# Another written-out order of all steps, with other early loads and fewer constant products

## The chip, the cores and the metric

The kernel runs on one NeuronCore of a Trainium2 chip. Five engines work side by side, each with its own instruction queue that runs in order: TensorE (PE; its weight loads are listed apart, as PEld), VectorE (DVE), ScalarE (ACT), GpSimd (POOL) and SyncE (SP), which here only issues DMA transfers. The metric is the time of one execution on the device in microseconds (us).

## What is computed

A recurrence over 768 time steps for 4 x 8 heads of width 40 is followed by a feed-forward block with an exact GELU, d_model 320 and d_ff 2048:

```python
for t in range(S):
    y[:, :, t] = np.einsum('bhd,bhde->bhe', rt, state)
    Sa = np.einsum('bhde,bhe->bhd', state, at)
    state_decay = state * wt[:, :, None, :] - np.einsum('bhd,bhe->bhde', Sa, bt)
    state = state_decay + np.einsum('bhd,bhe->bhde', vt, kt)
...
x = y.transpose(0, 2, 1, 3).reshape(B * S, H * D)
h = x @ w_in
g = 0.5 * h * (1.0 + erf(h * inv_sqrt2))
return g @ w_out
```

The six inputs of the recurrence are 32-bit floats. The two weights come as 64-bit floats, so that each is 5.2 MB and has to be turned into 32-bit numbers on the chip.

## The kernel before

The time axis is cut into 12 chunks of 64 steps. Within a chunk the recurrence becomes matrix products, with the inverse of a triangular matrix for each of the 32 heads. Chunk c's result x goes through the feed-forward block while the following chunks are being prepared.

Every piece of work is a named step, a small Python function. The order in which steps are issued is written out by hand as one long list of names in the function `order`. The number behind the name is the chunk (for the conversion steps, the unit). The kernel walks through the list and performs each; a step puts its instructions at the end of the queues of the engines that it uses. So the place in the list fixes the order on every engine's queue at once, and also which of four PSUM banks a product gets: `take` gives out the bank that has been free longest, `drop` returns it, in the list's order. A step at the head of a queue that is not ready holds everything behind it on that queue. Semaphore waits between engines follow from what steps read and write.

```python
def perform(steps, token):
    name, *numbers = token.split(".")
    steps[name](*(int(n) if n.isdigit() else n for n in numbers))
...
    for token in order(NCH, NS):
        perform(steps, token)
```

The steps that matter here, by what they do:

- **Loads, on SP's queue.** `Lw`, `La`, `Lb`, `Lk`, `LV`, `Lr` load a chunk's rows of the inputs w, a, b, k, v, r (lines 417 to 476). `Lf` and `Lf5` load the 64-bit words of w_in (lines 512 and 522), in 20 pieces of 256 KB, named by block of rows, half and part; `Ls` loads those of w_out (line 545). `Ns` and `Nl` take the triangular matrices through DRAM into GpSimd's layout (lines 852, 860), `Is`, `If` and `Ij` bring the inverses back (lines 880, 887, 892). `ox` exchanges rows of x between partitions (lines 1130, 1133), `so` stores results (line 1294).
- **Preparing a chunk.** `lg` takes the logarithm of w (ScalarE, line 645), `wT` and `cu` are products with a triangle of ones (TensorE), `ew` and `ec` the exponentials of these (ScalarE, lines 670 and 688). `ec` writes the decays that `sb` (VectorE, line 730) and `sk` (GpSimd or VectorE, line 735) multiply into the rows of b and k. `ta`, `tb`, `tk`, `tr`, `tv` transpose; `sa`, `sn`, `kc`, `rc`, `vc` scale or copy what they give.
- **The triangular matrices.** `nm` is the product (TensorE), `nk` its masking (VectorE, line 811); likewise `vm` with `vk` and `am` with `ak`.
- **The inverse in the first chunk.** It is computed by squarings: `qm.0` to `qm.4` on TensorE, each followed by `qc` (ScalarE), `qz` and `qa` (VectorE); `qt` and `qi` prepare it, `ql` and `qx` end it.
- **The inverse in the other chunks.** GpSimd clears its tile (`iz`, line 864) and eliminates row by row (`ic`, lines 873 and 875, eight steps in a chunk). When the inverses of 32 x 32 blocks are back, `tc_` (VectorE, line 961), `jm`, `jc`, `km`, `kt0` and `kt1` join the blocks.
- **The chunk's result and state.** `av`, `xm`, `sm`, `pk`, `pb`, `ym`, `tm` on TensorE, `xc0`, `xc1`, `sc`, `oa`, `om`, `od`, `oc`, `tn`, `yc` on VectorE and ScalarE. `om` writes x.
- **The feed-forward block.** `mh` is x @ w_in (line 1185), eight steps of 20 products for a chunk, `ge` the GELU (line 1190). The product with w_out is `pm` (line 1301) in the first three chunks and later the seven products `m1` to `m7` of a Strassen scheme (line 1224) with sums `s1` to `s4`, `e1` to `e6`.
- **Conversion of the 64-bit words**, in units (0 to 9 for w_in, 10 to 25 for w_out). Exponent and mantissa are taken apart by `cp`, `cm`, `cs` (VectorE) and `ce` (ScalarE), and put together in one of three ways: by `cv` alone (two VectorE instructions), by `cl`, `cn` (ScalarE) and `cg` (two GpSimd instructions), or, for unit 0, by `cx` on TensorE and `cy` on VectorE.
- **Products of constants.** `warm_first` (three) and `warm.4.i` (one each, 512 columns; i is only a label) multiply constants and nobody reads the result; they keep TensorE busy while it would wait.
- **Clearing of pads**: `pads_*`, `first_ones`, `Tt_zero`, `bias_set`, `unused` and the masks, nearly all on GpSimd.

Of the kernel before, what the change touches and what calls it, by code (L numbers as in the profile page):

```python
# [1339 lines left out]
```

## Time and profile before

| | |
|---|---|
| median of 3 runs | 688.01 us (685.67 to 690.76) |
| the profiled execution | 684.3 us, of which the span is 682.6 |
| TensorE busy | 652.3 us (96%) |
| VectorE, GpSimd, ScalarE busy | 385.2, 377.2, 236.9 us |
| mean granted TensorE clock | 0.989 |
| moved by DMA | 74.26 MB |

The page and the trace are of one execution. In rows of instructions, the first number is the start in us from the span's beginning, the second the duration; L1185 is a line of the kernel. In the brackets at the end stand the idle time of that engine just ahead of the row, and what ended it. The granted clock is the share of full speed that TensorE was given. "issue" is time in which an engine waited for nothing that the profile shows.

### The profile page before, as it was taken

The page shows a single profiled execution, that of the slowest core. Times are in us where ns is not written, and L with a number is a line of the kernel's source. Part 1 is how long each engine was busy: PE and PEld are TensorE (multiplying, and loading weights), DVE is VectorE, ACT ScalarE, POOL GpSimd, SP SyncE. Part 2 cuts the span into 40 slices and gives each one's busy share as a digit, 9 for nine tenths or more (in the row PEclk, how much of TensorE's full clock was granted, in tenths as well). Part 3 has the DMA queues.
Part 4 walks back from the last instruction along what each step waited for, and adds up shares of the span by engine and source line. Part 5 has one row for each costly group of instructions (what it writes and reads, how often), then busy time and mean ns, then how long its engine had stood idle before and what let it go on. Part 6 is the DMA issues. An engine that isn't in the chain of part 4 may idle for free.

```text
span 682.6 us, 29596 instructions
## 1 busy us (share of the span) xinstructions
PE 652.3 (96%) x13250; PEld 569.6 (83%) x13250; DVE 385.2 (56%) x483; ACT 236.9 (35%) x313; POOL 377.2 (55%) x796
## 2 busy tenths in 40 slices
PE   8687999999999999999989989999999999999997
PEld 4476887788778778998988988997998998998987
DVE  1868989750833645781852853753952763624403
ACT  4547535526222325322323332432342332132020
POOL 3445854853857705871883874864873863840000
PEclk9987999999999999999999999999999999999999
DMA  9987668758668746458547766656767153140100
GB/s 157 161 163 161 129 165 176 131 97 145 111 127 126 150 82 125 95 102 129 110 83 138 126 118 120 129 95 125 131 123 142 35 100 68 31 71 16 26 15 21
DMA packets 286043, 74.26 MB, mean 109 GB/s; under 512 B 265660, under 2 KB 280796, under 8 KB 285916
## 3 DMA queue, kind: packets, MB, share of 16 engines
q1 hardware_dynamic: 284852, 69.84, 55.2%
q0 software_dynamic: 864, 2.36, 2.0%
q8 instruction: 104, 1.70, 1.1%
q14 instruction: 23, 0.19, 0.1%
q10 hardware_dynamic: 200, 0.16, 0.1%
HBM read 58.69 MB, written 9.70 MB: 100 GB/s over the span
## 4 chain that ended last, share of the span: by engine, by line
PE 62%; POOL 14%; SPq 8%; DMA 6%; DVE 5%; issue 4%; ACT 1%; POOLq 0%; DVEq 0%
PE bank L1185 24%; PE bank L194 17%; PE bank L1224 14%; POOL tmp L873 7%; POOL W L875 6%; PE bank L1301 6%; SPq L417 2%; PE bank L697 1%; DMA w_out_sb<-in_moe_w_in_dram 1%; DMA Nb<-N_blocks 1%; DMA inv_blocks<-W 1%; SPq L522 1%; DVE conv L589 1%; SPq L887 1%; DMA r_pairs<-in_r_dram 1%
## 5 line engine op out<-in xcount | busy, mean ns | idle before, releaser
L1185 PE MATMUL bank<-xt,w_in_sb 64*128 64x256 f32 x1920 | 221.0, 383 | 1.8 <-issue 1.6
L873 POOL TENSOR_TENSOR tmp<-W,Nb 128x126 f32<-128x126 f32 (+22 forms) x341 | 152.7, 448 | 122.5 <-DMA Nb<-N_blocks 96.7
L1185 PEld LDWEIGHTS bank<-xt,w_in_sb 64*128 64x128 f32 x1920 | 185.7, 188 | 25.3 <-issue 4.2
L875 POOL TENSOR_TENSOR W<-W,tmp 128x126 f32<-128x126 f32 (+22 forms) x341 | 155.6, 456 | 26.7
L1190 ACT ACTIVATE gt<-bank 128x1024 f32<-128x1024 f32 x48 | 48.9, 1022 | 139.9 <-PE bank L1185 138.7
L1224 PE MATMUL bank<-w_out_sb,gt 128*128 128x160 f32 x576 | 82.8, 301 | 0.0
L1224 PEld LDWEIGHTS bank<-w_out_sb,gt 128*128 128x128 f32 x576 | 79.1, 190 | 1.3 <-issue 0.3
L1301 PE MATMUL bank<-w_out_sb,gt 128*128 128x320 f32 x192 | 54.9, 439 | 1.4 <-DVE w_out_sb L598 0.8
L1301 PEld LDWEIGHTS bank<-w_out_sb,gt 128*128 128x128 f32 x192 | 35.6, 190 | 16.4 <-DVE w_out_sb L598 1.3
L1062 DVE TENSOR_TENSOR SM<-bank,upper 128x832 f32<-128x832 f32 x24 | 23.7, 1016 | 29.2 <-PE bank L194 29.2
L961 DVE STREAM_TRANSPOSE conv<-Tt 128x512 f32<-128x512 f32 x11 | 7.8, 707 | 43.6 <-DMA Tt<-inv_blocks 43.5
L1112 DVE TENSOR_TENSOR st<-bank,st 128x832 f32<-128x832 f32 (+1 forms) x22 | 20.9, 985 | 16.8 <-PE bank L194 16.8
L1010 DVE COPY Tt<-bank 32x512 f32<-32x512 f32 x9 | 6.2, 689 | 41.6 <-ACT Tt L1010 41.5
L1177 DVE TENSOR_TENSOR os<-os,bank 128x160 f32<-128x160 f32 x36 | 11.5, 318 | 26.8 <-PE bank L1224 18.9
L1224 PE MATMUL bank<-extra,conv 128*128 128x160 f32 x176 | 26.0, 301 | 0.0
L1224 PEld LDWEIGHTS bank<-extra,conv 128*128 128x128 f32 x176 | 24.3, 190 | 0.5
L811 DVE TENSOR_TENSOR VR<-bank,upper 128x1024 f32<-128x1024 f32 x12 | 14.6, 1217 | 15.2 <-PE bank L194 15.1
L1177 DVE TENSOR_TENSOR conv<-gt 128x1024 f32<-128x1024 f32 x9 | 11.3, 1257 | 20.5 <-ACT gt L1190 20.4
L1043 DVE COPY SM<-bank 128x832 f32<-128x832 f32 x10 | 10.1, 1013 | 21.1 <-PE bank L194 21.1
L575 ACT ACTIVATE conv<-conv,rebias 128x320 uint32<-128x320 uint32 (+1 forms) x26 | 15.8, 619 | 18.0 <-DVE conv L568 17.9
L864 POOL MEMSET W<- 128x512 f32 x11 | 5.8, 529 | 29.1 <-DMA inv_blocks<-W 29.1
L1079 ACT COPY st<-bank 128x1024 f32<-128x1024 f32 x11 | 11.1, 1013 | 29.9 <-PE bank L194 29.9
(207 smaller groups left out, 1096.9 us busy)
## 6 DMA issues: line engine op xcount, KB each, us to landing
Nb<-N_blocks SPq DMA_DIRECT2D x22, 256.0 KB
b_rows<-in_b_dram SPq DMA_DIRECT2D x24, 160.0 KB
VR<-in_v_dram SPq DMA_DIRECT2D x24, 160.0 KB
k_rows<-in_k_dram SPq DMA_DIRECT2D x24, 160.0 KB
out_dram<-os SPq DMA_DIRECT2D x48, 80.0 KB
Tt<-inv_blocks SPq DMA_DIRECT2D x44, 64.0 KB
a_pairs<-in_a_dram SPq DMA_DIRECT2D x18, 144.0 KB
r_pairs<-in_r_dram SPq DMA_DIRECT2D x36, 72.0 KB
```

The lines of the kernel that those rows point to most:

```text
L194: nc.tensor.matmul(o, lhsT, rhs, start=first, stop=True, skip_group_check=True)
L575: nc.scalar.activation(power, power, ACT.Relu, bias=rebias, scale=8.0)
L811: nc.vector.tensor_tensor(to, pt, upper.unsqueeze(1).to_broadcast([P, NBL, C]), ALU.mult)
L873: nc.gpsimd.tensor_tensor(t, W[:, :rows, j:j + 1].to_broadcast([P, rows, rest]), Nb[:, j:j + 1, j + 1:].to_broadcast([P, rows, rest]), ALU ...
L875: nc.gpsimd.tensor_tensor(W[:, :rows, j + 1:], W[:, :rows, j + 1:], t, ALU.add)
L1062: nc.vector.tensor_tensor(SM[:, g], pair_of(f"S{c}_", g).rearrange("p x i c -> p i x c"), pass_upper.unsqueeze(1).unsqueeze(1).to_broadcas ...
L1112: nc.vector.tensor_tensor(to, pair_of(f"QY{c}_", g)[:, :, :, cols], to, ALU.add)
L1177: nc.vector.tensor_tensor(to, one_, other, how)
L1185: nc.tensor.matmul(ph[:, x, s], w_in_sb[half(x), kt, p * P:(p + 1) * P], xt[half(x), kt], start=kt == 0, stop=kt == NK - 1)
L1190: nc.scalar.activation(gt[:, 4 * q:4 * q + 4].rearrange("p (x s) t -> p x s t", x=2), bank(f"ph{c}_{q}").rearrange("p x (s t) -> p x s t", ...
L1224: nc.tensor.matmul(po[:, n, :DM // 2], l_[:, f], r_[:, f], start=f == 0, stop=f == NF // 2 - 1)
L1301: nc.tensor.matmul(po[:, g, :DM], gt[:, f, g * P:(g + 1) * P], w_out_sb[:, f], start=f == 0, stop=f == NF - 1)
```

## The change

Only the list in `order` is altered: nearly every line of it is another. No function is added or removed, and each step does what it did. Compared as lists:

- **Steps left out or added.** Before, eight single products of constants (`warm.4.` 20, 5, 29, 7, 24, 8, 1, 0); after, six (12, 5, 17, 10, 11, 20). Unit 1 of the conversion ends with `cl.1`, `cn.1`, `cg.1` instead of `cv.1`, unit 25 the other way round. All others, 1,470 of some 1,480, are in both lists.
- **The first loads.** Before, four pieces of w_in stand between w and b of the first chunk, and the rest of w_in lies among rows of the first two chunks. After, w.0, b.0 and w.1 come first, a.0 behind one piece, then the other pieces of the first part of w_in in one run, and b.1 and a.1 behind them.
- **The rest.** The engines' queues are reordered throughout, mostly by a few places.

The beginning of the list, cut:

```diff
-        pads_a.1 pads_a.0 Lw.0 Lf.0.1.0 lg.0 warm_set identity sums_mask first_ones.1 warm.4.20 warm_first
-        Lf.0.0.0 pads_w.1 bias_set pads_r.0 pads_extra.2 pads_extra.3 first_ones.0 pads_rows.1 pads_w.0
-        pads_extra.0 pads_rows.0 upper_mask pads_r.1 iz.1 pads_extra.1 cm.0 cn.0 wT.0 warm.4.5 cu.0 ec.0 cl.0
-        cx.0 ew.0 Lf.1.1.0 Lf.1.0.0 Lb.0 La.0 sb.0 cp.1 tb.0 cp.0 ce.0 sn.0 ta.0 sa.0 nm.0 Lw.1 Lb.1 Lf.2.1.0
-        Lf5.0.1 Lf.2.0.0 ce.1 lg.1 cm.1 nk.0 qi cu.1 wT.1 warm.4.29 ec.1 cs.0 cy.0 qt qm.0 cs.1 sb.1 cp.2 cm.2
+        pads_extra.0 sums_mask Lw.0 lg.0 cu.0 ec.0 pads_VR.0 identity Lb.0 warm.4.12 sb.0 tb.0 pads_w.0
+        first_ones.0 Lw.1 lg.1 warm_set bias_set pads_w.1 wT.1 pads_a.0 upper_mask pads_extra.1 Lf.3.0.0 La.0
+        Lf.2.0.0 wT.0 ew.1 ew.0 sn.0 pads_a.1 pads_r.0 ta.0 sa.0 nm.0 nk.0 qt qi Lf.0.1.0 Lf.1.0.0 Lf5.0.0
+        Lf.0.0.0 Lf5.0.1 Lf.1.1.0 cp.0 cu.1 ec.1 ce.0 cs.0 warm_first qm.0 cm.0 qc.0 cp.1 ce.1 cn.0 qz.0 cm.1
+        warm.4.5 Lf.2.1.0 cl.2 cn.1 cl.0 cs.1 qm.1 qa.1 qz.1 cx.0 Lf.3.1.0 cl.1 qc.1 Lb.1 La.1 qm.2 first_ones.1
...
```

Later places that the prediction speaks of. On GpSimd, before: `ic.5` (all) `Is.5 sk.5 iz.6`; `ic.6 Is.6 sk.6 iz.7`; `ic.7 Is.7 sk.7 iz.8 sk.8 ic.8`; `sk.9` inside `ic.9`; `Is.9 sk.10 iz.10 ic.10`. After: `sk.5` inside `ic.5`; `Is.5 sk.6 iz.6`; `Is.6 sk.7 iz.7`; `Is.7 iz.8 sk.8 ic.8`; `Is.8 iz.9 sk.9 ic.9`; `ic.10 Is.10 sk.10 iz.11`. On SP, before: `Is.1.0 Ns.2.1 Ls.13 Is.1.1 Ls.15 Nl.2.1 If.1.1 Ls.10 If.1.0`; after: `Is.1.0 Ls.13 Is.1.1 Ls.15 Nl.2.0 If.1.0 Nl.2.1 If.1.1 Ls.10`. And before: `Ns.7.1 If.6.1 If.6.0 Ij.6.0 so.4.0 Nl.7.0 Ij.6.1 Nl.7.1`; after: `so.4.1 Ns.7.0 Ns.7.1 Nl.7.0 Nl.7.1 Ij.6.1 If.6.1 If.6.0 LV.7 so.4.0`.

## The prediction

> **What bounds the kernel now.** I read the page's forty slices first, for the engine that never rests. Rows are TensorE's busy tenths, its granted clock and the share of the DMA engines.
>
> ```profile
> PE   8687999999999999999989989999999999999997
> PEclk9987999999999999999999999999999999999999
> DMA  9987668758668746458547766656767153140100
> ```
>
> TensorE is the bound from the fifth slice on: 652.3 us busy of a 682.6 us span. The change alters the set of products by two constants only, so it can win or lose just where TensorE waits or runs at a lower clock. Hence the second view, the start in windows of 4 us (window, length, busy time of PE, PEld, DVE, ACT, POOL, granted clock, DMA share, GB/s).
>
> ```profile
> 32.00:36.00 4.00, 1.33 (x81) 1.07 (x72) 1.74 (x2) 0.56 (x2) 3.30 (x4) 1.00 1.18 125
> 36.00:40.00 4.00, 4.00 (x74) 3.24 (x66) 2.75 (x4) 1.23 (x2) 0.40 (x1) 0.57 0.83 174
> ...
> 52.00:56.00 4.00, 2.20 (x128) 2.00 (x128) 4.00 (x5) 3.23 (x5) 2.05 (x3) 0.68 0.66 157
> 56.00:60.00 4.00, 3.32 (x84) 3.13 (x84) 3.51 (x6) 2.58 (x4) 0.60 (x1) 0.50 0.78 146
> ```
>
> Idle windows are followed by windows of a low clock: 4 x 0.43 + 4 x 0.32 + 4 x 0.50 = 5.0 us of TensorE's time gone. The timeline says who is late there: the first chunk's inversion, squaring after squaring (nm.0, qm.0, qm.1, qm.4).
>
> ```profile
> 18.61 1.16 PE L194 MATMUL bank<-aT,nT 40*64 40x64 f32 x64 [1.51 <-DVE aT L719]
> ...
> 24.62 1.19 PE L194 MATMUL bank<-N,st 32*32 32x32 f32 x116
> ...
> 30.95 1.58 PE L194 MATMUL bank<-turned,st 32*32 32x64 f32 x97
> ...
> 53.45 1.70 PE L194 MATMUL bank<-turned,st 32*32 32x32 f32 x108
> ```
>
> I summed TensorE's steps at their undisturbed durations (mh 2.2 us, pm 4.5, nm 1.05, and so on) in the old and the new order. The old order has done 34.5 us of work by 57.1 us, the new one stands within some 3 us of the old at nearly every milestone, and the whole is 629.6 us against 627.5. Next I looked at where the saturated stretch is met by a chain that is just in time: the second chunk's inversion, from GpSimd's last row to the product jm.1.
>
> ```profile
> 95.19 0.35 POOL L875 TENSOR_TENSOR W<-W,tmp 128x16 f32<-128x16 f32 x1
> 100.67 0.67 SPq L880 DMA_DIRECT2D inv_blocks<-W  x1
> 111.88 0.98 SPq L892 DMA_DIRECT2D T<-inv_blocks  x2
> 114.87 0.70 DVE L961 STREAM_TRANSPOSE conv<-Tt 128x512 f32<-128x512 f32 x1
> 115.62 0.75 PE L194 MATMUL bank<-conv,spare 32*32 32x32 f32 x64 [0.39 <-DVE conv L961]
> ```
>
> GpSimd was done at 95.5 and TensorE waited at 115.6: nearly all between is the SP queue. Last, the waits of the steady part. Only two have a releaser that is a step of the kernel and are over 1 us: both are `ec` (line 688), held by `sk` (line 735).
>
> ```profile
> 403.37 1.63 POOL L880 DMA_DIRECT2D inv_blocks<-W  x2 [0.30 <-POOL W L875]
> 404.95 1.60 POOL L735 TENSOR_TENSOR k_rows<-k_rows,part 128x640 f32<-128x640 f32 x1
> 406.59 0.70 ACT L688 ACTIVATE part<-bank 128x640 f32<-128x640 f32 x1 [5.33 <-POOL k_rows L735]
> 407.34 1.16 PE L194 MATMUL bank<-aT,nT 40*64 40x64 f32 x64 [1.74 <-ACT part L688]
> ```
>
> sk.7 sits behind all of ic.7; ec.8 must wait for it, and nm.8 needs the PSUM bank that ec.8 frees. The other is vm.7 behind ec.7 and sk.6, 1.76 us at 356.5. The clock then reads 0.92 and 0.91 in 400 to 410 and 410 to 420: 10 x (0.08 + 0.09) = 1.7 us more.
>
> **The change, part by part.** The profiled execution took 684.3 us, 1.7 over its span, and lies 3.7 under the median of 688.0. I add terms to it and carry the sum to the median.
>
> *Order of the loads.* Counting the SP queue, the new order has 0.64 MB issued up to b.0 (old 1.66), 0.96 up to w.1 (2.30), 1.54 up to a.0 (1.98), but 4.16 up to b.1 (2.62) and 6.27 up to v.0 (5.38); from the 76th issue on the two queues are level. Path to nm.0: lg.0 ends at 8.14 as before; cu.0 1.25; ec.0 0.70; then lg.1 with its table load 2.02, the exponential's table load 1.28, ew.1 and ew.0 2.0, sa.0 1.23. That is 16.7 against 18.61. nk.0 takes 1.22 more, `qi` on GpSimd 6.43, so qm.1 can start at 25.5 against 30.95. Further on the late rows end the lead's growth. The old queue passes 6.21 MB at 39.7, and a load of k took 5.3 us from issue to its reader (35.7 to 41.0), so v.0 is there at 45. tv.0 (1.97) and tk.0 (1.0) now stand ahead of qm.4, which starts at 48 instead of 53.5. Lead: 5 us. VectorE's conversions, begun at 8.3 us before, begin at about 21; what slides is 1.7 us of cp and cm, and unit 1 gives back 1.37 by passing to ScalarE and GpSimd (unit 25 returns 1.0 late, beside full TensorE work). I cost both at nothing: VectorE idles 3.6 us in 20 to 40 and 3.2 in 40 to 60. If that cover is gone, it is 1.7 us at most.
>
> *What of the lead reaches jm.1.* ic.1 took 33.4 us from 62.1 on; its input Nl.1.0 is the 67th issue instead of the 65th, 1.3 us later. Is.1.0 is the 118th instead of the 116th (+1.3), but the 2.5 us that the queue stood before xt's exchange (71.4 to 73.9, waiting for om.0) go with the lead: 99.5. From there the old queue needed 11.2 us to its last inverse load; the new one has Ls.13, Is, Ls.15, two Nl and the If together: Is.1.1 lands at 105.4, the If are out at 107.4, and with the 3.0 us between the old queue's last If (111.8) and tc_.1, jm.1 starts at 111.2: -4.4 us. TensorE's 85.5 us of work before it (86.5 before) is done by then. Bounds: -7 if GpSimd is also earlier, +4 if om.0 and nk.1, for which the queue now waits, are late.
>
> *Constants.* Eight single ones become six (the three of warm_first stay). Three of the eight stand in full stretches, at 60.1, 80.9 and 123.6 us, about 1.1 each by start to start; in the new order one does. Before jm.1 the chain decides, so only the one behind it counts: -1.0.
>
> *sk ahead of the inversion.* sk.6 to sk.9 move ahead of their ic, sk.5 into ic.5. Both ec waits go: -1.76 - 1.74 - 1.7 = -5.2 us. sk.10 goes behind ic.10 instead; ec.11 then holds a bank that mh.9.6 takes, with av.10 and ym.10 (2.5 us) between. I take nothing, at most 1.8.
>
> *What is late next.* TensorE arrives earlier at every jm. Their slack (from tc_'s start to jm's, less tc_) is small: chunk 2 0.8, 3 2.9, 4 0.9, 5 2.2, 7 1.4, 9 4.8. The work between nm and jm shrinks by 1.8 in chunk 2, 2.3 in 5, 2.2 in 7, 5.6 in 9. Chunk 2 waits 1.0. Chunk 5, with sk.5's 1.6 inside, 1.7. Chunk 7 would wait most, but its Nl, which stood behind so.4.0 and left at 363.5, now stands ahead of it and of the If: ic.7 can start some 6 us earlier. Chunk 9 has sk.9 out of its middle. Given back: +2.7.
>
> Sum: -4.4 - 1.0 - 5.2 + 2.7 = -7.9; 676.4 for a profiled run, **680 us** for the median.
>
> [...] The row: after the 2.67 us idle at 32.5 the clock was 0.57, and after 48 to 56, busy 2.2 to 2.3 of each 4 us with no idle over 1.7 us, 0.68 and 0.50. [...]
>
> **Rivals.**
> 1. *The clock falls more in the start.* With fewer constants and TensorE held at tv.0 from about 41 to 45 us, the low windows double: another 5.0 us. Against: the squarings stand closer. 688.0 - 7.9 + 5.0 = 685.
> 2. *The lead is lost on SP and GpSimd.* ic.1 starts no earlier and the queue is level from the 76th issue, so jm.1 stays at 115: 688.0 - 3.5 = 684.5. For it: GpSimd's 33.4 us and SP's unbroken issuing from 0 to 100 us. Against: 11.2 us from Is to the last load.
> 3. *Slower: the inversion ends last in every chunk whose window shrank.* Where Nl does not land before GpSimd is free, TensorE waits 1.0, 1.7, 4.3 (2.2 + 3.5 - 1.4) and 0.8 us in chunks 2, 5, 7 and 9, and the clock falls behind each as at 407, 4 x 1.7. With no gain at the start: 688.0 - 1.0 - 5.2 + 7.8 + 6.8 = 696. For it: Nl was what GpSimd waited for, 96.7 us in 10 waits. It decides from a Nl landing some 2 us later than now.
> 4. *Nothing changes*, each wait replaced by its like: 687. For it: TensorE's sequence is the old one within a few us nearly everywhere.
>
> **How the numbers follow.** Forecast 0.46 (own range 673 to 686), rival 1 0.12, rival 2 0.16, rival 3 0.20, rival 4 0.06. About 1% (6.9 us) is what a measurement of this kernel tells from no change, so faster is below 681.1 and slower above 694.9. Faster: some two thirds of the forecast and a quarter each of rivals 1 and 2, 0.38. Slower: rival 3 with a tenth of the rest, 0.27. The same: 0.35. The range leaves out a tenth on each side: 671 to 698.
>
> **What would show it.** qm.4 before 50 us and the If of chunk 1 out by 108 bear out the start; jm.1 at 115 or later with ic.1 ending at 97 or later is rival 2. No wait for ec over 1 us near vm.7 and nm.8 bears out the sk term; waits on tc_, Js or T in chunks 2, 5, 7 or 9 are rival 3. Clock under 0.9 in more than three windows before 64 us is rival 1. VectorE still converting w_in when mh.0 is due would make all of it wrong.

## The result and the profile after

The changed kernel takes 693.69 us (median of 20 runs, 686.84 to 699.21) beside 687.74 us for the kernel before in the same session: a ratio of 1.008, 95% interval [1.0061, 1.0099]. The forecast was 680, faster; it came out slower by 0.8%. The runs of the changed kernel lie further apart here, 12.4 us from end to end against 5.1, but in later sessions the kernel before spread by up to 13 us too. In the tables below a median is of all runs of a kernel and a ratio of its fast runs alone (within 1.5% of its fastest), so the two do not always agree, and the one profile of a slow run (without_two_nl9) is left out of the means. The profiled execution took 694.07 us, its span is 692.1 against 682.6, and the mean granted clock 0.979 against 0.989.

The forty slices of the page after (TensorE's busy tenths, its granted clock, DMA's share):

```profile
PE   4789899999999999999999999999998989999997
PEclk9996999999999999999999999999999999999999
DMA  9999578847569556559547757446755643130000
```

TensorE is still the bound, with 652.4 us of busy time as before (652.3), though it has two constants fewer: its products ran slower, not more of them. The clock's dip is deeper in slice 4 (52 to 69 us), and there is a new dent in TensorE's row at slices 31 and 33. These are the two places where the time went. The first, in windows of 4 us (columns as in the prediction):

```profile
32.00:36.00 4.00, 4.00 (x54) 1.58 (x57) 2.22 (x4) 0.59 (x1) 1.49 (x2) 0.61 0.75 150
...
52.00:56.00 4.00, 2.90 (x42) 1.34 (x46) 1.40 (x2) 1.80 (x4) 3.84 (x4) 0.52 0.91 110
56.00:60.00 4.00, 4.00 (x82) 2.38 (x77) 1.89 (x3) 1.35 (x3) 1.73 (x4) 0.50 0.79 145
60.00:64.00 4.00, 4.00 (x136) 3.82 (x134) 2.45 (x4) 1.48 (x3) 0.00 (x0) 0.50 0.81 187
...
92.00:96.00 4.00, 4.00 (x94) 3.40 (x88) 3.96 (x8) 1.04 (x2) 3.45 (x8) 0.64 0.69 194
```

Before, TensorE had one stretch of 6.8 us at half clock in the fifties (53.4 to 60.2); in windows of 0.2 us it now lasts 13.7 us, from 52.2 to 65.8 (the expectations below take it as 13.2), and another of 3.4 us comes at 93. From 53.1 on TensorE is full in these windows, so every us in them costs half a us. The timeline of TensorE shows how the stretch begins and what is done in it:

```profile
49.12 1.09 PE L193 MATMUL bank<-turned,st 32*32 32x32 f32 x104 [0.68 <-DVE turned L944]
53.10 0.54 PE L193 MATMUL bank<-turned,st 32*32 32x32 f32 x24 [2.89 <-issue]
53.57 2.08 PE L193 MATMUL bank<-cum_m,ident 128*128 128x512 f32 x2
55.57 1.99 PE L193 MATMUL bank<-aT,kT 40*64 40x64 f32 x64
57.49 2.07 PE L193 MATMUL bank<-cum_m,ident 128*128 128x512 f32 x2
```

qm.4 starts at 49.1, as early as forecast (48), but stops inside its 128 products for 2.89 us on "issue". Then follow two products of constants (one is two rows of the trace), am.0 and vm.0, each at nearly double length: a constant takes 2.08 us instead of 1.12. jm.1 starts at 120.46 instead of 115.62.

The second place is SP's queue while chunk 8 is being finished. First the kernel before, then after (start, duration, number of issues):

```profile
455.31 3.20 SPq L852 DMA_DIRECT2D N_blocks<-spare  x4
...
464.38 0.47 SPq L860 DMA_DIRECT2D Nb<-N_blocks  x1
464.90 1.24 SPq L1294 DMA_DIRECT2D out_dram<-os  x2
466.18 0.60 SPq L860 DMA_DIRECT2D Nb<-N_blocks  x1
```

```profile
466.21 2.05 SPq L851 DMA_DIRECT2D N_blocks<-spare  x4
468.30 1.04 SPq L891 DMA_DIRECT2D T<-inv_blocks  x2
469.39 1.17 SPq L1293 DMA_DIRECT2D out_dram<-os  x2
470.67 3.99 SPq L439 DMA_DIRECT2D w_tile<-in_w_dram  x4
474.77 2.25 SPq L859 DMA_DIRECT2D Nb<-N_blocks  x2
```

Ns.9 (N_blocks) now stands behind the inverse loads If.8, and Nl.9 (Nb) behind the stores so.6.0 and the loads Lw.10 as well, so Nl.9 leaves at 474.8 instead of 464.4. GpSimd waits 14.94 us for it (7.73 before) and starts ic.9 at 480.6 instead of 470.3 (GpSimd's first row of ic.9, before and after):

```profile
470.27 0.24 POOL L873 TENSOR_TENSOR tmp<-W,Nb 128x31 f32<-128x31 f32 x1 [7.73 <-DMA Nb<-N_blocks]
```

```profile
480.61 0.24 POOL L872 TENSOR_TENSOR tmp<-W,Nb 128x31 f32<-128x31 f32 x1 [14.94 <-DMA Nb<-N_blocks]
```

Two waits of TensorE come of it, the second in part, as will be shown (VectorE's row first, then TensorE's two):

```profile
524.12 0.71 DVE L960 STREAM_TRANSPOSE conv<-Tt 128x512 f32<-128x512 f32 x1 [10.10 <-DMA Tt<-inv_blocks]
...
525.80 0.75 PE L193 MATMUL bank<-conv,spare 32*32 32x32 f32 x64 [2.73 <-DVE SM L1042]
564.47 10.43 PE L1184 MATMUL bank<-xt,w_in_sb 64*128 64x256 f32 x80 [2.59 <-ACT part L687]
```

The first of TensorE's is jm.9: VectorE had stood 10.10 us for the inverse (tc_.9), with the copy that the bracket names behind it. The second is mh.9.6, which needs the bank that ec.11 frees, which waits for sk.10 behind all of ic.10. Behind each the clock reads 0.83, in the windows 520 to 530 and 560 to 570, which is 1.7 us each. The two waits and the two dips come to 2.7 + 2.6 + 1.7 + 1.7 = 8.7 us, most of what is lost in this part.

The middle did get faster. The table gives the starts of jm as read from TensorE's timeline of several kernels, and what lies between; in each column the order of the steps is either that of before (b) or that of after (a).

| kernel | jm.1 | jm.2 to jm.7 | jm.7 to jm.11 | jm.11 to the end |
|---|---|---|---|---|
| before | 115.6 b | 254.5 b | 203.2 b | 60.5 |
| after | 120.5 a | 250.4 a | 216.1 a | 60.5 |
| after, second profile | 121.8 a | 249.0 a | 214.4 a | 60.5 |
| start_of_after | 121.7 a | 254.3 b | 203.2 b | 60.5 |
| start_of_before | 116.9 b | 251.7 a | 215.5 a | 60.5 |
| middle_of_after | 116.7 b | 248.5 a | 204.7 b | 60.5 |
| only_nl9 | 118.2 a | 251.3 a | 210.7 a, Nl.9 early | 60.5 |
| two_constants_later | 117.6 a, constants moved | 250.3 a | 214.8 a | 60.5 |
| both_kept_ns | 115.7 a, constants moved | 249.2 a | 207.1 a, Ns.9 and Nl.9 early | 60.5 |

The new order has less work done by jm.1, jm.2 and jm.7 (1.0, 4.3 and 4.3 us, counted with undisturbed durations as in the prediction), so starts alone flatter it in the first half. Against work done it lies 5.8 us behind at jm.1, 4.9 at jm.2, 0.9 at jm.7 and 11.6 at the end; less the 2.1 us of constants left out, that is the 9.5 us between the spans. So, in this profile: some 5 lost in the start, 4.0 won from jm.2 to jm.7, 10.7 lost from there on.

### The profile page after: what moved, and what is told of

The parts are those of the page before. It is cut to its first block, busy times and chain, and to the rows that moved or that the text cites. A ratio compares the mean times of both kernels' runs of the same rounds, so it can differ in the third digit from the quotient of the medians.

```text
span 692.1 us, 29580 instructions
## 1 busy us (share of the span) xinstructions
PE 652.4 (94%) x13246; PEld 569.4 (82%) x13246; DVE 388.2 (56%) x483; ACT 240.6 (35%) x316; POOL 377.7 (55%) x796
## 4 chain that ended last, share of the span: by engine, by line
PE 70%; POOL 10%; DVE 6%; issue 5%; DMA 4%; SPq 3%; ACT 2%; DVEq 0%; POOLq 0%; ACTq 0%
PE bank L1184 24%; PE bank L193 22%; PE bank L1223 16%; PE bank L1300 8%; POOL tmp L872 4%; POOL W L874 4%; PE bank L696 2%; DMA inv_blocks<-W 1%; SPq L886 1%; DMA T<-inv_blocks 1%; DVE conv L588 1%; DVE conv L581 1%; DMA Tt<-inv_blocks 1%; DMA w_tile<-in_w_dram 1%; DMA Nb<-N_blocks 1%
## 5 line engine op out<-in xcount | busy, mean ns | idle before, releaser
L960 DVE STREAM_TRANSPOSE conv<-Tt 128x512 f32<-128x512 f32 x11 | 7.8, 708 | 45.4 <-DMA Tt<-inv_blocks 45.4
L1223 PE MATMUL bank<-extra,gt 128*128 128x160 f32 x144 | 21.2, 300 | 0.0
L734 POOL TENSOR_TENSOR k_rows<-k_rows,part 128x640 f32<-128x640 f32 x8 | 13.2, 1651 | 14.3 <-ACT part L687 13.2
L193 PEld LDWEIGHTS bank<-SM,Tt 64*64 64x64 f32 x768 | 17.5, 133 | 3.4 <-issue 3.4
```

The lines of the kernel that those rows point to most:

```text
L193: nc.tensor.matmul(o, lhsT, rhs, start=first, stop=True, skip_group_check=True)
L1223: nc.tensor.matmul(po[:, n, :DM // 2], l_[:, f], r_[:, f], start=f == 0, stop=f == NF // 2 - 1)
```

## The experiments

All ratios are to the kernel before on the same chip, in the same session. Each kernel ran twelve times (sk10_early and after_again six times) beside 29 or 35 runs of the kernel before.

| kernel | median, us | ratio, 95% interval |
|---|---|---|
| start_of_before | 687.73 | 1.0037 [1.0010, 1.0064] |
| start_of_after | 689.72 | 1.0072 [1.0044, 1.0101] |
| middle_of_after | 683.54 | 0.9977 [0.9947, 1.0008] |
| sk10_early | 706.32 | 1.0303 [1.0265, 1.0342] |
| without_two_constants | 686.67 | 1.0031 [0.9997, 1.0065] |
| constants_together | 689.88 | 1.0079 [1.0050, 1.0108] |
| sk10_inside | 691.28 | 1.0062 [1.0027, 1.0096] |
| nl9_early * | 686.87 | 0.9997 [0.9964, 1.0031] |
| after_again | 695.27 | 1.0105 [1.0066, 1.0144] |
| old_start_nl9_early * | 687.84 | 1.0003 [0.9970, 1.0036] |
| only_nl9 | 687.91 | 0.9997 [0.9966, 1.0028] |
| two_constants_later | 690.06 | 1.0017 [0.9983, 1.0050] |
| both_mended * | 686.71 | 0.9953 [0.9926, 0.9980] |
| without_two_nl9 * | 688.83 | 0.9969 [0.9935, 1.0003] |
| start_of_after_later | 688.50 | 0.9986 [0.9958, 1.0014] |
| both_kept | 686.06 | 0.9963 [0.9928, 0.9999] |
| both_kept_ns | 683.98 | 0.9916 [0.9880, 0.9952] |
| old_start_only_nl9 | 685.33 | 0.9942 [0.9907, 0.9978] |

In the four with a star Ns.9 stands ahead of nk.9, which writes what it reads: chunk 9's inverse is made there from the matrix of an earlier chunk, and Ns.9 does not wait for its own. What that does to the time is shown below.

### Where: old and new order spliced

**start_of_before** has the list of before up to mh.0, then all other steps in the order of after.

```diff
-        pads_extra.0 sums_mask Lw.0 lg.0 cu.0 ec.0
...
-        cv.23 tv.2 mh.0.5 mh.0.6 mh.0.7
+        pads_a.1 pads_a.0 Lw.0 Lf.0.1.0 lg.0
...
+        ge.0.1 mh.0.0 mh.0.1 mh.0.7 mh.0.4 mh.0.5
```

> The old order up to the end of mh.0, then the new order of what is left. Theory: the new order loses 5.8 us on TensorE before mh.0 starts (94.1 us with 60.4 us of work done, old 91.2 with 63.4), most of it in a low clock from 52 to 66 us, and some 9 us from chunk 9 on; then this takes 693.7 - 5.8 = 688 us. Rival: what is lost in the start would have been waited for later anyway, at the inverses; then 692 to 694.

**start_of_after** is the other way round: the list of after up to mh.0, the order of before behind it.

```diff
-        pads_a.1 pads_a.0 Lw.0 Lf.0.1.0 lg.0
...
-        ge.0.1 mh.0.0 mh.0.1 mh.0.7 mh.0.4 mh.0.5
+        pads_extra.0 sums_mask Lw.0 lg.0 cu.0 ec.0
...
+        cv.23 tv.2 mh.0.5 mh.0.6 mh.0.7
```

> The mirror: the new order up to the end of mh.0, then the old order of what is left. Theory: the loss is in the start, 687.7 + 5.8 less one constant of 1.0 = 692.5 us, with a window of half clock between 50 and 66 us in its trace. Rival: the loss lies in the later part alone; then 687 to 688.

**middle_of_after** has only the steps from jm.2 to jm.7 in the new order.

```diff
-        tc_.2 jm.2 jc.2 tk.3 km.2 mh.1.3
...
-        xc0.7 mh.6.4 mh.6.0 jm.7
+        tc_.2 jm.2 LV.3 La.4 ta.4 cu.4 jc.2 km.2
...
+        xc0.7 ge.6.3 mh.6.2 jm.7
```

> The old order up to jm.2, the new one from there up to jm.7, the old one for the rest; no constant changes its place. Theory: between jm.2 and jm.7 the new order wins 4 us on TensorE (its lag, counted against the work done, falls from 4.9 to 0.9 us), because ec.7 and ec.8 no longer wait for sk.6 and sk.7: 687.7 - 4 = 683.5 us, without waits for ec at vm.7 and nm.8. Rival: TensorE then waits for the inverse at jm.8 or jm.9 instead: 687.

The kernel before took 684.65 us on this chip, so the ratios count. The new start with the old rest came out at 1.0072, the old start with the new rest at 1.0037, and neither interval holds 1: both halves lose. The first is what its theory gave (692.5 us is 1.007); the second lies between its theory (688 us, 1.000) and its rival (692 to 694). The middle alone gave 0.9977, between its theory (0.994) and its rival (0.999), with 1 inside the interval; its profile has 6 us less from jm.2 to jm.7 and no wait for ec there.

### The end: sk.10, or Nl.9

**sk10_early** puts sk.10 ahead of ic.10, where it stood before.

```diff
-        Is.10.0.p Is.10.1.p sk.10.p ox.9.1
+        Is.10.0.p Is.10.1.p ox.9.1
...
-        nm.11 cu.11 ic.10.0.4
+        nm.11 cu.11 sk.10.p ic.10.0.4
```

> The new order with one step moved: sk.10 ahead of ic.10 instead of behind it. Theory: the wait of 2.6 us for ec.11 at mh.9.6 and the low clock behind it (0.83 over 10 us, 1.7 us) go: 693.7 - 4.3 = 689.4 us. Rival: the inverses of chunks 10 and 11 come later by the 1.6 us that sk.10 takes and TensorE waits there instead: 693.

It took 1.0303, the worst of all, against both expectations. GpSimd's timeline says why:

```profile
539.59 1.54 POOL L737 TENSOR_TENSOR k_rows<-k_rows,part 128x640 f32<-128x640 f32 x1 [17.60 <-DMA k_rows<-in_k_dram]
```

The new order loads Lk.10 only behind Lr.11 and Lw.11, at 534.6 us in the kernel after, where the old one does at 488.9. sk.10 waited 17.60 us at the head of GpSimd's queue with ic.10 behind it, and TensorE then stood 15.1 us at jm.10. In the new order sk.10 and Lk.10 belong together: one can't be moved forward without the other.

**sk10_inside** puts it into the middle of ic.10.

```diff
-        ic.10.0.4 ic.10.4.8 ic.10.8.12 ic.10.12.16 ic.10.16.20 ic.10.20.24 ic.10.24.28 ic.10.28.31
-        Is.10.0.p Is.10.1.p sk.10.p
+        ic.10.0.4 ic.10.4.8 ic.10.8.12 ic.10.12.16 ic.10.16.20 sk.10.p ic.10.20.24 ic.10.24.28 ic.10.28.31
+        Is.10.0.p Is.10.1.p
```

> The kernel after, with sk.10 on GpSimd inside the inversion of chunk 10 (ahead of its sixth instruction, as sk.9 stood in the kernel before) instead of behind it. By then Lk.10 should have landed. In the kernel after mh.9.6 waited 2.59 us for ec.11 behind sk.10, and the clock fell to 0.83 in the ten us behind it. Theory one, this wait is what the end of the run loses: the wait goes, the lag against the kernel before grows by 2 to 3 us in chunk 10 instead of 5.8, and the time is 689 to 690. Rival, TensorE only reaches the next wait (tc_.10) earlier because the inversion of chunk 10 now ends 1.8 us later: jm.10 starts as late as in the kernel after and the time stays at 693 to 694.

1.0062 against 1.0080 and 1.0105 for the kernel after (on other chips) can't be told from no gain. In its profile the wait for ec.11 is gone, and a wait of 4.6 us for tc_ (line 964) stands there instead, as the rival had it: the inversion was late anyway.

**nl9_early** moves four steps on SP's queue.

```diff
-        so.6.1 LV.9 Lk.9 mh.7.4 nm.9 xm.8 mh.7.5 If.8.1 If.8.0 nk.9 xc1.8 tk.9 kc.9 tc_.8 tv.9 Ns.9.1 Ns.9.0
+        so.6.1 LV.9 Lk.9 mh.7.4 nm.9 xm.8 mh.7.5 Ns.9.1 Ns.9.0 If.8.1 If.8.0 nk.9 xc1.8 tk.9 kc.9 tc_.8 tv.9
...
-        mh.7.1 mh.7.2 mh.7.3 so.6.0 Lw.10 Nl.9.1 Nl.9.0 Lr.10
+        mh.7.1 mh.7.2 mh.7.3 Nl.9.1 Nl.9.0 so.6.0 Lw.10 Lr.10
```

> The kernel after, with Ns.9 ahead of If.8 and Nl.9 ahead of so.6.0 and Lw.10 on SP's queue; nothing else moves. In the kernel after Nl.9 issues at 474.8 and 476, 10 us later than before, tc_.9 waits for the inversion that starts from it, and jm.9 waited 2.73 us. Theory one, this queue is the cause: ic.9 starts 6 to 10 us earlier, jm.9 does not wait, and the time is 689 to 690. Rival, ic.9 is held by what stands ahead of it on GpSimd (iz.9, sk.8, ic.8), or If.8 now comes later and tc_.8 with it: the time stays at 693 to 695.

**only_nl9** makes the second of these moves alone.

> The kernel after, with Nl.9 ahead of so.6.0 and Lw.10 on SP, but Ns.9 where the change has it, behind If.8. If the four issues of so.6.0 and Lw.10 (469.4 to 474.7 in the kernel after) are the cause, Nl.9 issues at 470 instead of 474.8, jm.9 waits 0 or little, and the time is 686 to 687, as with both moves. If Ns.9 behind If.8 is the larger part (it issues at 466.2 against 449.7 with both moves), Nl.9 still comes some 8 us late, jm.9 still waits 1 us or more and the time is 689 to 690.

only_nl9 gives 0.9997, and against the kernel after on its chip (1.0105) that is 1.1%, some 7 us (against the 1.0080 of the result 0.8%, between 5 and 6 us), for two issues moved ahead of six (each ratio within some 0.35%). Nl.9 leaves at 469.1, 5.6 us earlier, and neither wait is left: jm.9 waits for nothing, mh.9.6 for 0.9 us, and the clock does not fall. Its SP timeline and TensorE's windows of 10 us:

```profile
467.52 1.00 SPq L895 DMA_DIRECT2D T<-inv_blocks  x2
469.13 1.13 SPq L863 DMA_DIRECT2D Nb<-N_blocks  x2
470.32 1.86 SPq L1297 DMA_DIRECT2D out_dram<-os  x2
```

```profile
520.00:530.00 10.00, 10.00 (x224) 8.26 (x224) 2.08 (x3) 2.25 (x4) 7.44 (x23) 1.00 0.54 101
...
560.00:570.00 10.00, 9.27 (x180) 8.13 (x180) 1.84 (x2) 3.26 (x4) 0.77 (x3) 1.00 0.57 106
```

So the wait for ec.11 in the kernel after came mostly from the late Nl.9: ic.10 stood behind a late ic.9, and sk.10 behind both. The place of sk.10 has a share as well, since old_start_only_nl9 (below), with Nl.9 early, still waits 2.2 us for ec.11.

nl9_early came to the same ratio with a shorter path for Ns.9 and a new wait: nk.9 can't overwrite the tile until Ns.9 has read it, and TensorE's mh.7 needs the bank that nk.9 frees. It waits 2.4 to 3.4 us for it in all four starred kernels, and in no other. The line of VectorE in both_mended:

```profile
460.46 1.23 DVE L814 TENSOR_TENSOR spare<-bank,upper 128x1024 f32<-128x1024 f32 x1 [11.37 <-DMA N_blocks<-spare]
```

From jm.7 to jm.11 seven profiles with the new order and Nl.9 late have 214.1 us in the mean (210.9 to 216.1; sk10_early, with 226.3, is not among them), the four with it early and its own matrix 209.2 (207.1 to 210.7). Three profiles with the old order from jm.2 on have 203.2, 203.2 and 206.0, to which 2.2 us belong that the new order has still to do at jm.7. So some 5 of 8 us lost there are found; what the rest is was not tried.

### The start: constants and the clock

**without_two_constants** leaves out the two constants at 53.57 and 57.49.

```diff
-        qm.4 warm.4.10 am.0 Lf5.1.1
+        qm.4 am.0 Lf5.1.1
...
-        qa.4 ql vc.0 warm.4.11
-        vm.0 ak.0
+        qa.4 ql vc.0 vm.0 ak.0
```

> The kernel after, without the two products of constants behind qm.4 and vc.0 (warm.4.10 and warm.4.11); four remain, nothing else moves. In the kernel after they ran at half the clock, 2.08 and 2.07 us each, in a stretch of 13.2 us in which TensorE was busy and the granted clock stayed at half. Theory one, the constants only stand in the path: jm.0 comes 4 us earlier, the clock is lower for the same 13.2 us or a little less, jm.1 starts at 117 instead of 120.5 and the time is 690 against 693.7. Rival, the constants are what brings the clock back: the half clock lasts longer than 13.2 us, to 70 us or further, jm.1 stays at 120 or later and the time stays at 693 to 696.

**constants_together** puts these two and a third in a row.

```diff
-        qm.4 warm.4.10 am.0
+        qm.4 warm.4.10 warm.4.11 warm.4.20 am.0
...
-        qa.4 ql vc.0 warm.4.11
+        qa.4 ql vc.0
...
-        pk.0 warm.4.20 tk.1
+        pk.0 tk.1
```

> The kernel after, with three of its six products of constants (warm.4.10, warm.4.11, warm.4.20) in one row right behind qm.4 instead of spread over qm.4, vc.0 and pk.0. If products of the full array, several in a row, bring the clock back sooner than the small products between them, the half clock ends by 60 us instead of 65.6, and jm.1 starts at 117 to 118; the time is 690 to 691. If the length of the half clock does not depend on which products keep TensorE busy, it lasts 13.2 us (52.4 to 65.6) as in the kernel after, with 1 us more of constants inside it, and the time stays at 693 to 695.

**two_constants_later** moves the two to where TensorE waits for VectorE later on, and where the kernel before had one.

```diff
-        qm.4 warm.4.10 am.0
+        qm.4 am.0
...
-        ql vc.0 warm.4.11
+        ql vc.0
...
-        sb.2 tb.2 ta.2 sn.2
+        sb.2 warm.4.10 tb.2 ta.2 sn.2
...
-        ym.1 yc.1 nm.2 xm.1
+        ym.1 yc.1 warm.4.11 nm.2 xm.1
```

> The kernel after, with the two products of constants behind qm.4 and vc.0 (warm.4.10 and warm.4.11) moved on TensorE to ahead of tb.2 and ahead of nm.2, where TensorE waited 0.94 and 1.17 us for VectorE and where the kernel before had a constant. Theory: there they stand beside a wait and keep TensorE busy, so that the clock doesn't halve at 92 to 97; the time is that without the two (686.7) less 0 to 1.6, so 685 to 687. Rival: constants in a wait do nothing for the clock, or the wait only moves: 688 to 690, the two constants cost what they last.

Without the two the ratio is 1.0031 instead of 1.008, 3.4 us less (the kernel after itself was not timed on that chip); they run in the path, 2 x 2.08 us. In its profile the half clock isn't longer (54.9 to 65.1), but jm.1 starts at 119.8 and not at 117. In their later places the ratio is 1.0017 instead of 1.0105, some 6 us with the same number of constants, 4 us against 1.008. There the second of them stands in the wait, at full clock, and the window behind reads 1.00 where the kernel after had 0.64 (TensorE's timeline and window):

```profile
88.91 1.13 PE L197 MATMUL bank<-cum_m,ident 128*128 128x512 f32 x2 [0.75 <-DVE aT L722]
```

```profile
92.00:96.00 4.00, 4.00 (x59) 3.54 (x50) 3.96 (x8) 0.23 (x1) 3.44 (x8) 1.00 0.75 195
```

Over all profiles, the clock fell between 85 and 102 us in seven of the ten that have no constant near this wait, and in none of the ten that have one (five with the old start, five with the constants moved).

In a row (constants_together) the three ran from 54.0 for 4.16 us, most of it at half clock, and the clock was back at 56.7 instead of 65.8. But TensorE then came to av.0 before VectorE was ready and stood from 61 for 1.2 us, the clock was at half again from 63.5 to 70.3 and from 90.8 to 97.6, and the time stayed at 1.0079. The two readings, both from that kernel:

```profile
54.01 4.16 PE L197 MATMUL bank<-cum_m,ident 128*128 128x512 f32 x6
```

```profile
56.00:60.00 4.00, 4.00 (x133) 2.50 (x131) 0.61 (x1) 1.40 (x3) 2.23 (x4) 0.91 0.71 142
```

**after_again** is the changed kernel unchanged, for a second profile.

> The kernel after, unchanged, as the base of the other runs on this chip and for a second profile of it. If nothing but the order sets its time, the ratio is 1.006 to 1.010 here too (689 to 691 where the kernel before takes 684.7). If the stretches of half clock in its first 110 us fall differently from execution to execution, this profile shows other stretches than 31.7 to 35, 52.4 to 65.6 and 92 to 97, but the wait of jm.9 and that of mh.9.6 for ec.11 again.

The half clock lies elsewhere in it (32.1 to 38.9 and 56.0 to 73.1), the two late waits are there again (3.1 and 4.0 us). In all twenty profiles each stretch of half clock before 110 us lasts a whole multiple of 3.41 us: 3.4, 6.8, 10.2, 13.7, 17.1 or 20.5 (3.41 from 31.71 and 13.65 from 52.19 in the kernel after, 3.41 from 36.34 and 6.83 from 53.41 in the kernel before). The start therefore has to be compared over several executions. From 10 to 110 us, adding up (1 - granted clock) over windows of 1 us, the seven profiles with the new start give 6.8 to 17.1 us of clock lost, 11.4 in the mean, and 12.2 us of idle TensorE; the five with the old start 5.1 to 8.5, 7.1 in the mean, and 13.8 idle; the five with the constants moved 6.8 to 10.2, 7.8 in the mean, and 13.9 idle.

**start_of_after_later** makes the same move in start_of_after, where the end is the old one.

```diff
-        qm.4 warm.4.10 am.0
+        qm.4 am.0
...
-        ql vc.0 warm.4.11
+        ql vc.0
...
-        sb.2 tb.2 ta.2 sn.2
+        sb.2 warm.4.10 tb.2 ta.2 sn.2
...
-        ym.1 yc.1 nm.2 xm.1
+        ym.1 yc.1 warm.4.11 nm.2 xm.1
```

> The new order up to mh.0 and the old order behind it (start_of_after, which measured 1.0072), with the two products of constants moved to ahead of tb.2 and of nm.2. Here SP's queue of chunk 8 is the old one, so only the start can differ from the kernel before. If the start's loss is the two constants that stand at half clock on the path (4.1 us), the ratio falls to 1.001. If the start loses because the clock is lower for longer whatever stands there, it stays at 1.006 to 1.008.

0.9986 instead of 1.0072 (on another chip): with nothing else changed in the start, its loss is gone. By the times, what the new start lost is the place of two constants. The profiles show only a part of it: jm.1 starts at 120.4 in the mean of the seven with the new start (116.6 to 125.0), at 118.0 in the five with the constants moved and at 116.1 in the five with the old start, which has 1.0 us more work by then. Where the rest of the 6 us is won was not found.

### Do the two add?

**old_start_nl9_early** is start_of_before with the four moves of nl9_early.

```diff
-        nk.9 xc1.8 tk.9 kc.9 tc_.8 tv.9 Ns.9.1 Ns.9.0
+        nk.9 xc1.8 tk.9 kc.9 tc_.8 tv.9
...
-        so.6.0 Lw.10 Nl.9.1 Nl.9.0 Lr.10
+        Nl.9.1 Nl.9.0 so.6.0 Lw.10 Lr.10
```

> The order of before up to mh.0, the order of after behind it, and Ns.9 and Nl.9 ahead of If.8 and of so.6.0 and Lw.10 on SP. Theory: the change loses in two places that have nothing to do with each other, the start (the clock) and SP's queue in chunk 8; both are undone here and what is left is the gain of chunks 2 to 7 (about 5 us between jm.2 and jm.7). The two ratios measured, 1.0037 for the old start with the new rest and 0.992 for the four transfers moved in the kernel after, give 0.9954, that is 681.5, faster than both kernels. Rival: the four transfers gained more than their wait only because of the executions it was timed in; then 684 to 685.

1.0003 instead of 0.9954: a miss.

**both_mended** has two_constants_later's and nl9_early's moves together, **without_two_nl9** leaves the two constants out instead.

```diff
-        qm.4 warm.4.10 am.0
+        qm.4 am.0
...
-        so.6.0 Lw.10 Nl.9.1 Nl.9.0 Lr.10
+        Nl.9.1 Nl.9.0 so.6.0 Lw.10 Lr.10
```

> The kernel after with both suspected causes undone and nothing else: the two products of constants moved behind tb.2's and ahead of nm.2's wait (as in two_constants_later), and Ns.9 and Nl.9 ahead on SP (as in nl9_early). If the whole loss of the change is these two (the two constants at half clock on the path in the start, the late Nl.9 at the end), what is left is the gain of chunks 2 to 7: the ratios measured alone against the kernel after on the same chips, 0.991 each, give 1.009 x 0.991 x 0.991 = 0.991, faster than both kernels. Rival, the two are one: what one of them wins the other can't win again, as the old start with the early Nl.9 showed (1.0003 where 0.9954 was expected): then 0.998 to 1.001.

> The kernel after without the two products of constants behind qm.4 and vc.0, and with Ns.9 and Nl.9 ahead on SP. If the two losses add: 1.0031 less 0.008 is 0.995, a little above both_mended if the constants at their later places keep the clock up, equal to it if they do nothing. If the two are one: 0.998 to 1.001.

0.9953 and 0.9969 lie between the sum and the rival. None of these three tells it, since the wait of mh.7 for nk.9 is new in them, and in the profile of old_start_nl9_early it cost 3.0 us. So the question was put again with the matrix kept.

**both_kept** is two_constants_later with the move of only_nl9. **both_kept_ns** has Ns.9 ahead of If.8 as well, but behind nk.9. **old_start_only_nl9** is start_of_before with the move of only_nl9.

```diff
-        mh.7.5 If.8.1 If.8.0 nk.9 xc1.8 tk.9 kc.9 tc_.8 tv.9 Ns.9.1 Ns.9.0
+        mh.7.5 nk.9 Ns.9.1 Ns.9.0 If.8.1 If.8.0 xc1.8 tk.9 kc.9 tc_.8 tv.9
...
-        so.6.0 Lw.10 Nl.9.1 Nl.9.0 Lr.10
+        Nl.9.1 Nl.9.0 so.6.0 Lw.10 Lr.10
```

> The kernel after with the two products of constants ahead of tb.2 and nm.2 (as in two_constants_later) and Nl.9 ahead of so.6.0 and Lw.10 (as in only_nl9); every step still reads what it reads in the kernel after. It stands in for both_mended, in which Ns.9 was put ahead of nk.9 and so read the matrix of an earlier chunk, without waiting for nk.9 (the same in nl9_early, old_start_nl9_early and without_two_nl9). If the wait for nk.9 mattered little, as only_nl9 (0.9997) against nl9_early (0.9997) suggests, this is at 0.994 to 0.997, faster than the kernel before. If both_mended was fast because that wait was missing, it is at 0.998 to 1.001.

> As both_kept, and Ns.9 directly behind nk.9 with If.8 behind Ns.9 on SP, as in the kernel before, so Ns.9 waits for nk.9 and If.8 with it. In the kernel after nk.9 starts at 459.5 and Ns.9 issues at 466.2. If the place of Ns.9 is part of the loss, ic.9 starts 3 us or more earlier than in both_kept and the time is 1 to 2 us less, 0.992 to 0.995. If only Nl.9's place counts, or If.8 and tc_.8 come late in exchange, it is the same as both_kept or slower, 0.995 to 0.999.

> start_of_before with Nl.9 ahead of so.6.0 and Lw.10, and Ns.9 where it was, so that chunk 9's matrix is its own. If the two losses of the change add, the start being that of before and the queue mended, 1.0037 less 0.008 to 0.011 gives 0.993 to 0.996. If they do not, it is at 1.000 as old_start_nl9_early was (1.0003).

They add in the old start: with the mended queue it gives 0.9942, inside the 0.993 to 0.996 of the sum, and its interval leaves out the rival's 1.000. both_kept gives 0.9963, as expected, but its interval reaches 0.9999, so it alone would not rule the rival out, and it lies above the plain sum (0.991). With Ns.9 in its old place as well it is 0.9916 [0.9880, 0.9952], faster than both kernels, by 0.8% than before and by 1.6 to 1.9% than after. Ns.9's place may be worth something too; the two intervals overlap. SP's queue and the page of both_kept_ns:

```profile
454.84 2.04 SPq L855 DMA_DIRECT2D N_blocks<-spare  x4
456.99 3.08 SPq L890 DMA_DIRECT2D Tt<-inv_blocks  x4
460.11 0.98 SPq L895 DMA_DIRECT2D T<-inv_blocks  x2
461.20 1.13 SPq L863 DMA_DIRECT2D Nb<-N_blocks  x2
```

```profile
PE   4887899999999999999999999999999999999997
PEclk9896999999999999999999999999999999999999
```

Nl.9 leaves at 461.2, ic.9 starts at 466.0 (480.6 in the kernel after), and from slice 6 on TensorE's row has no dent.

## Why the prediction was wrong, point by point

- **The early path: right within 1.7 us.** nm.0 17.8 us (16.7 forecast), qm.1 27.2 (25.5), the transposes of v.0 at 45.4 (45), qm.4 49.1 (48).
- **jm.1 earlier by 4.4 us: wrong, it is 4.8 later. This step failed.** It followed the second chunk's inversion to its input and took TensorE's own 85.5 us of work as done by then. The inversion did not start by Nl.1: GpSimd is held at 70.2 by a conversion (cg.7) whose VectorE part stands behind sk.1, and starts ic.1 at 71.8 instead of 62.1.

```profile
70.22 1.59 POOL L620 TENSOR_TENSOR w_in_sb<-conv 128x512 f32<-128x512 f32 x1 [1.43 <-DVE conv L588]
71.77 0.69 POOL L872 TENSOR_TENSOR tmp<-W,Nb 128x31 f32<-128x31 f32 x1
```

  So ic.1 ended at 104.9, where rival 2's sign was 97 or later, and the last If left at 111.3 to 112.4, where 107.4 was forecast; with the prediction's own 3.0 us behind it jm.1 could have started at some 116 (an estimate), so by that this alone takes the 4.4 us. (The 3.0 us were counted from 111.88, which is Ij, line 892. The last If left at 110.8, and VectorE came to tc_.1 without a wait in both kernels, so its own queue is part of that time.) Even that did not set jm.1: its input was ready at 119.6, and TensorE came to it at 120.5 without a wait (VectorE's row, then TensorE's):

```profile
118.87 0.71 DVE L960 STREAM_TRANSPOSE conv<-Tt 128x512 f32<-128x512 f32 x1
...
120.46 0.84 PE L193 MATMUL bank<-conv,spare 32*32 32x32 f32 x64
```

  What set it is rival 1, priced at 5.0 us, and its sign is there (four windows of 4 us before 64 us are under 0.9): the clock lost 10.2 us by jm.1 in this profile against 5.1, and 11.4 against 7.1 over the profiles above. With 5.1 us less of it TensorE would still have come at 115.4 (an estimate), not at 111.2: it idled 14.0 us from 10 to 110 us, against 14.3 before, so the lead of qm.4 went into other waits. Rival 1's chance was too small, and the argument for it (fewer constants) only half right: two of the constants stood in the path at half clock, and one was missing at a later wait.
- **Constants, -1.0: wrong in sign.** The term counted constants only where TensorE was full, and nothing for where the others were put. By the times their place is worth some 6 us (two_constants_later against after_again, and again start_of_after_later against start_of_after).
- **sk ahead of the inversion, -5.2: right in mechanism.** The waits for ec at vm.7 and nm.8 (1.76 and 1.74 us) are gone, and the middle wins 4.0 us against work done; jm.2 to jm.7 takes 249.2 us in the mean of sixteen profiles with the new order there and 253.9 in three with the old.
- **Given back, +2.7: near in size, wrong in place, and chunk 9 missed. The second step that failed.** The waits on tc_ and T come to 3.3 us (chunk 6 0.25, chunk 7 1.23 and 1.06, chunk 8 0.76); chunks 2 and 5 have none. Chunk 9 was taken as free because sk.9 left its middle; the place of its Ns and Nl on SP was not looked up. This is rival 3's mechanism, which was said to decide from an Nl landing 2 us late: it came 10 us late, in that one chunk, and cost 5 to 7 us.
- **sk.10, nothing, at most 1.8: wrong in this kernel,** 2.6 us of wait and the clock behind it. It mostly goes when Nl.9 is early: with sk.10 where it is, only_nl9 and both_kept wait 0.9 us and both_kept_ns not at all, but old_start_only_nl9 2.2.
- **The length of the half clock: not in the forecast.** In the profile after, TensorE was busy without a gap from 53.1, and the clock stayed at half until 65.8, for 12.7 us; before, the longest stretch lasted 6.8 us in all. What ends such a stretch was not shown.

## What to carry to other kernels

A filler product is worth what its place makes it: at a wait it cost little here (1.0017 with the two moved there, 1.0031 without them) and the clock stayed up (1.00 in the window behind), behind a stall it ran at half speed on the path (2.08 us). When a whole order is exchanged, read each queue for each repeated chain, not only where a step is known to be tight: two issues that stood behind six others cost more (5 to 7 us) than five chunks had gained (4.0). A step moved on one engine needs its load moved on the other (sk.10 without Lk.10: 2% slower than the kernel after).

## What was not expected of the hardware

"issue" stops TensorE mostly at the same products of the program, from one execution to the next: of the fifteen profiles with the new start, with or without the two constants in place, all stop with 24 products of qm.4 left, fourteen with 6 of qm.1 and eleven with 3 of qm.0, for 0.2 to 4.7 us. Between these places lie 127 and 508 products, that is one and four times 127, each with its weight load. The windows of the kernel after between the stops (columns as above; x counts the products), and two lines of its page:

```profile
25.20:31.40 6.20, 3.24 (x127) 2.24 (x128) 2.79 (x4) 4.00 (x7) 3.89 (x8) 1.00 1.09 136
31.40:53.05 21.65, 17.95 (x508) 13.39 (x507) 17.58 (x24) 11.79 (x17) 9.33 (x9) 0.90 0.94 161
```

```profile
PE 652.4 (94%) x13246; PEld 569.4 (82%) x13246; DVE 388.2 (56%) x483; ACT 240.6 (35%) x316; POOL 377.7 (55%) x796
...
q8 instruction: 104, 1.70, 1.1%
```

The first of the queues named "instruction" moved 104 packets of 16 KB (1.70 MB), and TensorE's 2 x 13,246 instructions over 104 are 255 a packet (an estimate; the page does not say whose packets they are); 127 products with their weight loads are 254. The longest stops, 2.89 and 2.31 us in the kernel after, fall in the first 60 us, and the DMA share reads 1.09 and 0.94 in the two windows above. Whether TensorE waits there for such a packet was not tried.

The other surprise is the clock: 13.7 us at half speed under a busy TensorE when the products are of tiles of 64x64 and smaller with single constants between, 3.4 when three constants of 128x512 stand in a row. The kernel after has a stretch of 3.4 us too, from 31.7, with little but products of 128x512 in it. That the size of the tiles decides is suggested by these profiles and not shown: no run changed it alone.
